# A spectral layer and two MLPs on one core: the second chunk of the first MLP by blocks

## The chip, the cores and the metric

One core of a Trainium2 chip runs the whole program. The metric is the device time of one execution, in microseconds. The kernel before took 1215.2 us (median of three runs, 1214.34 to 1215.99).

## The reference

Three steps follow one another on 2 x 3008 tokens of 256 features, in float32:

```python
X = np.fft.rfft(x, axis=1)                       # over the 3008 tokens
Yr = Xr @ w_r - Xi @ w_i + b_r
Yi = Xr @ w_i + Xi @ w_r + b_i
Yr, Yi = soft_threshold(Yr, 0.01), soft_threshold(Yi, 0.01)
x = np.fft.irfft(Yr + 1j * Yi, n=3008, axis=1)   # to 6016 x 256
h = x @ w_in1;  x = (h * sigmoid(h)) @ w_out1    # 256 -> 2048 -> 256
h = x @ w_in2;  out = max(0.01 * h, h) @ w_out2  # 256 -> 2048 -> 256
```

The MLP weights arrive as float64 words; the kernel reads them as pairs of 32-bit words and rebuilds float32 values on chip.

## The kernel before, in words

**Precision.** Every float32 operand of a matmul is split into a high part (hi, a cast) and a low part (lo, the difference). A product is three matmuls: lo·hi, hi·lo, hi·hi.

**Stages.** A first transform makes a_sb. Then 48 spectral items run, one call of spectrum(j) for each j; the stages of several items overlap in one call (STAGES lists them with their lag, in the order in which each engine gets them): threshold, split_a, split_z, split_y, store, mix, forward, backward. mix writes a PSUM bank pz, forward py, backward pb; store copies pb to SBUF as bo and sends it to a scratch tensor in HBM. inverse reads that back (bt) and writes px, from which the token columns (ring) are split. The last five calls of spectrum lie inside the first iterations of the MLP loop.

**MLP loop.** The tokens are cut into 12 chunks, 11 of 512 and one of 384. Per layer and chunk there are 8 pairs; a pair holds two slices of 128 hidden columns. Iteration i of the loop issues, in program order: for the pair before (one) parts of its preparation; first(0) of pair i; the products "1" of pair i-2 (two); one step of preparation for the next chunk (make_next, a px of the inverse in layer 1); first(1); the products "a" and "b" of pair i-2; the last preparation of pair i-1; and behind all that the weight work (split_w, then sums_w1). Pairs 0 to 7 are chunk 0, 8 to 15 chunk 1, 16 to 23 chunk 2. first(s) is six matmuls of 512 columns into a bank ph.

**Plain and by blocks.** A plain pair splits both activated slices and multiplies them with four 128 x 128 weight blocks: 12 matmuls of 512 columns, issued one iteration later. A pair by blocks uses Strassen's scheme in Winograd's form: seven products of 256 columns instead of eight, each three matmuls, so 21 matmuls of 256 columns, issued two iterations later. It needs sums of the activations (t1 on POOL; t23 and t4 on DVE) and seven weights (S1 to S4, A11, A12, A22). In the kernel before, chunks 0 and 1 of layer 1 are plain and the others by blocks (the last is a tail of its own).

**Weights.** The pieces of the first layer's weights are loaded (L116, wraw), begun (ACT L123 and L125, DVE L128 and L130), scaled (DVE L135), added (POOL L142) and split (ACT L149, POOL L150). In the spectral stage fifth does parts of a piece behind each item; in chunk 0 step does one piece behind each first. The sums of the block weights come later: sums_w1(p) at the end of iteration 8 + p (POOL L470 and four L457), split_w at the end of iteration 9 + p (four casts on ACT, L463; four differences on DVE, L464, called wlo).

**Activation and preparation.** Behind first(s) ACT computes a tanh (L520) and DVE finishes the activation (L521). Of a pair by blocks, POOL makes t1 (L538) and la (L526), DVE t23 (L545), l (L526), t4 (L552) and lb (L526, 768 columns), ACT the casts h, ha and hb (L564).

**Order and waits.** The program fixes the order on every engine as it is written; each engine takes its instructions in that order, and one that waits holds back what stands behind it. All of PSUM is two pools of four banks: ps_h (ph, py, px) and ps_a (pa, pz, pb and the sums acc). A new tile of a pool waits for the readers of the tile whose bank it takes.

Of the kernel before, what the change touches and what calls it, by code (L numbers as in the profile page):

```python
# [9 lines left out]
F32 = mybir.dt.float32  # L10
# [61 lines left out]
def spectral_mlp_kernel(ctx, tc, x, w_r, w_i, b_r, b_i, w_in1, w_out1, w_in2, w_out2, da, ea, dm, out):  # L72
# [7 lines left out]
    near = dict(reuse_waits="tile")  # L80
    dram = pool("dram", 1, space=bass.MemoryType.DRAM)
    ps_h = pool("ps_h", 4, space=bass.MemoryType.PSUM)
    ps_a = pool("ps_a", 4, space=bass.MemoryType.PSUM)
    const = pool("const", 1)
    stage = pool("stage", 3)

# [9 lines left out]
    def weight_pieces(win, wout, in_dst, out_dst):  # L96

        win, wout = win.bitcast(U32), wout.bitcast(U32)
        pieces = []
        for q in range(NF // 2 + 1):
            if q < NF // 2:
                for d in range(2):
                    pieces.append((win[d * 128:(d + 1) * 128, q * 512:(q + 1) * 512], [w[:, d * DFF + q * 256:d * DFF + (q + 1) * 256] for w in in_dst]))
            if q:
                for f in (2 * q - 2, 2 * q - 1):
                    pieces.append((wout[f * 128:(f + 1) * 128, :], [w[:, f * D:(f + 1) * D] for w in out_dst]))
        loaded, begun, scaled, rounded, made = [], [], [], [], []  # L110

        def load():
            if pieces:
                src, dst = pieces.pop(0)
                raw = raws[0].tile([128, 512], F32, tag="wraw", name="wraw", bufs=3 if raws[1:] else 2).bitcast(U32)
                nc.sync.dma_start(out=raw, in_=src)  # L116
                loaded.append((raw.rearrange("p (e w) -> p e w", w=2), dst))

        def begin():
            raw, dst = loaded.pop(0)  # L120
            m = stage.tile([128, 256], U32, tag="wm", name="wm", bufs=2)
            c = stage.tile([128, 256], F32, tag="wc", name="wc", bufs=4).bitcast(U32)
            nc.scalar.activation(out=c, in_=raw[:, :, 0], func=ACTF.Copy, scale=2.0 ** -29)  # L123

            nc.scalar.activation(out=m.bitcast(F32), in_=raw[:, :, 1].bitcast(F32), func=ACTF.Copy, scale=2.0 ** -112)  # L125
            yield

            nc.vector.tensor_scalar(out=m.bitcast(F32), in0=m.bitcast(F32), scalar1=MAG, scalar2=-MAG, op0=ALU.min, op1=ALU.max)  # L128
            yield
            nc.vector.tensor_scalar(out=m, in0=m, scalar1=3, scalar2=0x7FFFFFFF, op0=ALU.logical_shift_left, op1=ALU.bitwise_and)  # L130
            begun.append((raw, m, c, dst))

        def scale():
            raw, m, c, dst = begun.pop(0)
            nc.vector.scalar_tensor_tensor(out=m, in0=raw[:, :, 1], scalar=0x80000000, in1=m, op0=ALU.bitwise_and, op1=ALU.bitwise_or)  # L135
            yield
            scaled.append((m, c, dst))

        def around(add):
            m, c, dst = scaled.pop(0)  # L140
            r = dst[0].bitcast(U32) if len(dst) == 1 else c
            add.tensor_tensor(out=r, in0=c, in1=m, op=ALU.add)  # L142
            rounded.append((c.bitcast(F32), dst))

        def split():
            c, dst = rounded.pop(0)
            if len(dst) == 2:
                hi, lo = dst
                nc.scalar.copy(hi, c)  # L149
                nc.gpsimd.tensor_tensor(out=lo, in0=c, in1=hi.bitcast(F32), op=ALU.subtract)  # L150
            made.append(1)

        def step():

            if scaled:
                around(nc.gpsimd)
            parts = [p() for p, ready in ((scale, begun), (begin, loaded and len(begun) < 2)) if ready]
            done = len(rounded)
            while parts:
                for p in list(parts):  # L160
                    if next(p, parts) is parts:
                        parts.remove(p)
            for _ in range(done):
                split()
            if scaled:
                around(nc.gpsimd)
            load()

        def fifth(i):

            if i in (0, 3):
                if rounded:
                    split()
                if loaded and not begun:
                    list(begin())
            elif i in (1, 4) and begun:
                list(scale())
            if i in (2, 4) and scaled:
                around(nc.gpsimd)
                load()  # L180

        def until(n):
            while len(made) < min(n, 2 * NF):
                step()

        return load, step, fifth, until
# [41 lines left out]
    with tc.tile_pool(name="xp", bufs=6) as xp:  # L228
# [20 lines left out]
            load_x(c)  # L249
        wms = xp.tile([128, 2, 2, D], F32, name="wms", bufs=1)  # L250
        for c in range(R2 // NA):
            pa = [ps_a.tile([128, 512], F32, tag="acc", name="pa") for _ in range(2)]
            for s in range(NA):
                for h in range(2):
                    nc.tensor.matmul(  # L255
                        pa[h][:, s * 128:(s + 1) * 128],
                        lhsT=xt[c][:, s, h * 128:(h + 1) * 128],
                        rhs=da_sb,
                        start=True,
                        stop=True,  # L260
                        skip_group_check=True,
                    )
            xt.pop(c)
            load_x(c + 5)
            for h in range(2):
                (nc.vector.tensor_copy if h and c > 14 else nc.scalar.copy)(
                    a_sb[:, h, :, c * NA:(c + 1) * NA], pa[h].rearrange("p (s j) -> p j s", s=NA)[:, :NJ])
            if c in (6, 7):
                nc.sync.dma_start(out=wms[:, :, c - 6, :], in_=(w_r, w_i)[c - 6].rearrange("(h p) e -> p h e", p=128))
            elif c == 8:  # L270
                braw = xp.tile([128, D], F32, name="braw", bufs=1)
                nc.vector.memset(braw, 0.0)
                for p in (0, 32, 64, 96):
                    nc.sync.dma_start(out=braw[p:p + 1, :], in_=(b_r, b_i)[p // 32 % 2].rearrange("(o e) -> o e", o=1))
                nc.vector.memset(pick.bitcast(F32), 0.0)
                for p in (0, 32, 64, 96):
                    nc.vector.memset(pick[p:p + 1, p // 32 % 2 * 64:][:, :64].bitcast(F32), 1.0)
            elif c == 10:
                load_dm(0)
            elif c == 11:  # L280
                load_dm(2)
            elif c == 12:
                nc.scalar.copy(bias, braw)
                nc.vector.tensor_tensor(out=bias[64:], in0=braw[64:], in1=bias[64:].bitcast(F32), op=ALU.subtract)
                nc.scalar.copy(wm["hi"], wms)
                nc.vector.tensor_tensor(out=wm["lo"], in0=wms, in1=wm["hi"].bitcast(F32), op=ALU.subtract)
                nc.sync.dma_start(out=ea_sb, in_=ea)
            elif c == 13:
                split_dm(0)
            if c > 13:  # L290
                load_w()
# [12 lines left out]

    def mix(j):
        hi, lo = a_t.pop(j)
        pz = ps_a.tile([128, 512], F32, tag="acc", name="pz")
        terms = [(u, v, h) for u, v in ((hi, wm["lo"]), (lo, wm["hi"]), (hi, wm["hi"])) for h in range(2)]
        for n, (u, v, h) in enumerate(terms):
            nc.tensor.matmul(pz, lhsT=u[:, h, :], rhs=v[:, h].rearrange("p g e -> p (g e)"),  # L310
# [12 lines left out]
    def forward(j):  # L323
        zh, zl = z_t.pop(j)
        dh, dl = dm_t[j]
        py = ps_h.tile([128, 512], F32, tag="h", name="py")[:, :D]
        terms = [(u[:, 64 * (1 - g):64 * (3 - g)], v[:, g, :]) for u, v in ((dl, zh), (dh, zl), (dh, zh)) for g in range(2)]
        for n, (u, v) in enumerate([(pick, bias)] + terms):
            nc.tensor.matmul(py, lhsT=u, rhs=v, start=(n == 0), stop=(n == len(terms)))  # L329
# [17 lines left out]
    def backward(j):  # L347
        yh, yl = y_t.pop(j)
        dh, dl = dm_t.pop(j)
        pb = ps_a.tile([128, 512], F32, tag="acc", name="pb")[:, :D]  # L350
        for n, (u, v) in enumerate(((dl, yh), (dh, yl), (dh, yh))):
            nc.tensor.matmul(pb, lhsT=u[:, 192:], rhs=v, start=(n == 0), stop=(n == 2))  # L352
        b_p[j] = pb
# [30 lines left out]
    for j in range(n_items - 1):  # L384
        spectrum(j)
        if j == n_items - KH + KT + 6:
            load_b()
            load_b()
        fifth_w(j % 5)
    right.close()  # L390


# [3 lines left out]
    at = lambda t: t % RING  # L396
    accs, x2f, late = {}, {}, {}

    def inverse(h):

        g, n, bt = bts[0]
        px = ps_h.tile([128, 512], F32, tag="h", name="px")
        for s in range(n):
            nc.tensor.matmul(px[:, s * PAIR:(s + 1) * PAIR], lhsT=bt[:, s, h * 128:(h + 1) * 128],  # L404
                             rhs=ea_sb, start=True, stop=True, skip_group_check=True)
# [25 lines left out]
    def ahead(layer, c):  # L431
# [3 lines left out]
        steps = []  # L435
        while made[0] < sum(CHUNKS[c]):
            made[0] += sizes.pop(0) * PAIR
            steps += [lambda h=h: inverse(h) for h in range(2)]
        return steps


# [41 lines left out]
    class Pair:  # L483
# [4 lines left out]
        def __init__(self, layer, c, p):  # L488
            self.layer, self.c, self.p = layer, c, p
            self.t0, self.n = CHUNKS[c]  # L490
            self.mode = "plain" if layer == 1 and c < 2 else "blocks" if self.n == 512 else "tail"
            self.ph = {}

        def first(self, s):
# [79 lines left out]
        def acc(self, i):  # L574
            key = self.layer, self.c, i
            if key not in accs:
                accs[key] = ps_a.tile([128, 512], F32, tag="acc", name="acc")
            return accs[key]

        def products(self, which):  # L580
# [70 lines left out]
    for i in range(len(pairs) + 2):  # L651
# [9 lines left out]
        def between(f):  # L661
            if f < 10 and f % 2 == 0:
                spectrum(n_items + 1 + f // 2)
            if 0 < f < NF:
                step_w()
            if f == 6:
                raws.pop(0)
            if f == 9:
                fs.close()
                late["m2"] = pool("late", 2, **near)  # L670
                late["m4"] = pool("late4", 2, **near)
# [93 lines left out]
```

## Time and profile before

| | |
|---|---|
| median of the runs | 1215.2 us |
| profiled execution | 1214.85 us |
| its span | 1213.1 us |
| PE busy | 1196.0 us (99%) |
| DVE busy | 842.3 us (69%) |
| ACT busy | 782.3 us (64%) |
| POOL busy | 567.2 us (47%) |

The span runs from the first to the last instruction; the rest of the execution's time lies around it. A busy time is the time in which an engine runs at least one instruction. Matmuls overlap in the pipeline, so the distance between two starts says more than the duration of one. In the trace the MLP loop begins at 167.92 us, chunk 1 at 222.32 us and chunk 2 at 268.90 us.

### The profile page before, as it was taken

The numbers are of one execution on the slowest core, as the hardware profiler recorded it, in microseconds if no ns is written. First come the engines' busy times: TensorE is split into PE (matmuls) and PEld (weight loads), VectorE is DVE, ScalarE is ACT, GpSimd is POOL, SyncE is SP. The second block draws the span as 40 slices with busy tenths as digits, with TensorE's granted clock in tenths as the row PEclk, the third lists the DMA queues.
The fourth block names the chain that finished last, engine by engine and source line by source line (L and its number), as shares of the span: only waits on it lengthen the run. The fifth ranks groups of instructions, "written<-read, shape, count | busy, mean of one in ns | idle before, by whom it ended". The sixth has DMA issues, their size and how long they took to land.

```text
span 1213.1 us, 20072 instructions
## 1 busy us (share of the span) xinstructions
PE 1196.0 (99%) x7346; PEld 1071.5 (88%) x7346; DVE 842.3 (69%) x1525; ACT 782.3 (64%) x1614; POOL 567.2 (47%) x606
## 2 busy tenths in 40 slices
PE   9999998999999999999999999999999999999998
PEld 9888886888999999989999988988888898888898
DVE  0798877768889888888988895555555455555543
ACT  4898866656666666666665776656656665665664
POOL 0334524543444444444545575555545455554532
PEclk9999999999999999999999999999999999999999
DMA  9344443001112111101100110110011011001000
GB/s 218 111 125 129 139 138 101 32 14 48 51 31 64 57 40 49 58 26 55 45 26 19 35 32 1 35 36 31 5 36 36 1 35 36 28 9 35 32 1 31
DMA packets 35882, 61.60 MB, mean 51 GB/s; under 512 B 3908, under 2 KB 15784, under 8 KB 35784
## 3 DMA queue, kind: packets, MB, share of 16 engines
q1 hardware_dynamic: 35784, 60.33, 16.2%
q8 instruction: 57, 0.93, 0.3%
q14 instruction: 41, 0.34, 0.1%
HBM read 41.70 MB, written 18.61 MB: 50 GB/s over the span
## 4 chain that ended last, share of the span: by engine, by line
PE 91%; DVE 3%; ACT 2%; DMA 2%; issue 1%; SPq 0%; ACTq 0%; DVEq 0%
PE ph L501 41%; PE acc L571 37%; PE pz L310 4%; PE py L329 2%; PE pa L255 2%; PE px L404 2%; DVE wlo L464 1%; PE pb L352 1%; DMA wraw<-in_moe_w_out_dram 1%; DMA bt<-scr 0%; ACT bo L358 0%; DMA xt<-in_x_dram 0%; DVE py L337 0%; DVE ph L521 0%; DMA wraw<-in_moe_w_in_dram 0%
## 5 line engine op out<-in xcount | busy, mean ns | idle before, releaser
L526 POOL TENSOR_TENSOR la<-u,ha 128x512 fp32r<-128x512 f32 (+1 forms) x176 | 232.8, 1323 | 246.7 <-ACT ha L564 245.7
L526 DVE TENSOR_TENSOR lb<-u,hb 128x768 fp32r<-128x768 f32 (+1 forms) x176 | 178.2, 1012 | 220.7 <-ACT hb L564 219.0
L501 PE MATMUL ph<-xhi,winlo 128*128 128x512 f32 (+1 forms) x768 | 240.3, 394 | 5.5 <-DVE la L526 5.5
L501 PE MATMUL ph<-xlo,winhi 128*128 128x512 f32 (+1 forms) x768 | 239.1, 391 | 1.2 <-POOL xlo L427 1.2
L501 PE MATMUL ph<-xhi,winhi 128*128 128x512 f32 (+1 forms) x768 | 237.6, 391 | 0.0
L520 ACT ACTIVATE u<-ph 128x512 f32<-128x512 f32 (+1 forms) x192 | 113.8, 593 | 139.2 <-PE ph L501 139.2
L501 PEld LDWEIGHTS ph<-xlo,winhi 128*128 128x128 f32 x768 | 144.0, 188 | 36.3 <-POOL xlo L427 5.5
L501 PEld LDWEIGHTS ph<-xhi,winhi 128*128 128x128 f32 x768 | 143.8, 188 | 30.8
L538 POOL TENSOR_TENSOR u<-u 128x256 f32<-128x256 f32 x160 | 126.0, 787 | 64.9 <-DVE u L521 58.4
L564 ACT CAST hb<-u 128x768 fp32r<-128x768 f32 (+1 forms) x176 | 140.4, 798 | 9.4 <-DVE u L552 4.9
L571 PE MATMUL acc<-lb,whi 128*128 128x256 f32 (+1 forms) x496 | 141.1, 284 | 0.0
L571 PE MATMUL acc<-hb,whi 128*128 128x256 f32 (+1 forms) x496 | 139.6, 281 | 0.0
L571 PE MATMUL acc<-hb,wlo 128*128 128x256 f32 (+1 forms) x496 | 139.5, 281 | 0.0
L501 PEld LDWEIGHTS ph<-xhi,winlo 128*128 128x128 f32 x768 | 120.5, 189 | 9.1 <-DVE la L526 6.2
L523 ACT ACTIVATE ph<-ph 128x512 f32<-128x512 f32 (+1 forms) x96 | 55.1, 574 | 113.0 <-PE ph L501 113.0
L521 DVE SCALAR_TENSOR_TENSOR ph<-u,ph 128x512 f32<-128x512 f32 (+1 forms) x112 | 76.5, 683 | 64.4 <-ACT u L520 64.4
L564 ACT CAST ha<-u 128x512 fp32r<-128x512 f32 (+1 forms) x176 | 109.7, 623 | 14.7 <-POOL u L538 14.7
L526 DVE TENSOR_TENSOR l<-ph,h 128x512 fp32r<-128x512 f32 (+1 forms) x176 | 117.2, 666 | 0.0
L545 DVE TENSOR_TENSOR u<-ph,u 128x512 f32<-128x512 f32 x160 | 109.0, 681 | 6.3 <-POOL u L538 6.3
L564 ACT CAST h<-ph 128x512 fp32r<-128x512 f32 (+1 forms) x176 | 102.4, 582 | 2.7 <-DVE ph L521 1.6
L571 PE MATMUL acc<-ha,whi 128*128 128x256 f32 (+1 forms) x352 | 102.1, 290 | 0.0
L571 PE MATMUL acc<-la,whi 128*128 128x256 f32 (+1 forms) x352 | 100.9, 287 | 0.0
(123 smaller groups left out, 2669.0 us busy)
## 6 DMA issues: line engine op xcount, KB each, us to landing
wraw<-in_moe_w_in_dram SPq DMA_DIRECT2D x32, 256.0 KB
wraw<-in_moe_w_out_dram SPq DMA_DIRECT2D x32, 256.0 KB
scr<-bo SPq DMA_DIRECT2D x48, 128.0 KB
scr<-x2o SPq DMA_DIRECT2D x22, 256.0 KB
x2i<-scr SPq DMA_DIRECT2D x22, 256.0 KB
out_dram<-x2o SPq DMA_DIRECT2D x22, 256.0 KB
dmr<-in_dm_dram SPq DMA_DIRECT2D x34, 160.0 KB
bt<-scr SPq DMA_DIRECT2D x14, 384.0 KB
```

The costliest lines, as they stand in the source:

```text
L255: nc.tensor.matmul(pa[h][:, s * 128:(s + 1) * 128], lhsT=xt[c][:, s, h * 128:(h + 1) * 128], rhs=da_sb, start=True, stop=True, skip_group_ ...
L310: nc.tensor.matmul(pz, lhsT=u[:, h, :], rhs=v[:, h].rearrange("p g e -> p (g e)"), start=(n == 0), stop=(n == len(terms) - 1))
L329: nc.tensor.matmul(py, lhsT=u, rhs=v, start=(n == 0), stop=(n == len(terms)))
L501: nc.tensor.matmul(ph, lhsT=u[:, h, f * 128:(f + 1) * 128], rhs=v[:, h, :], start=(i == 0), stop=(i == len(terms) - 1))
L520: nc.scalar.activation(out=th, in_=ph, func=ACTF.Tanh)
L521: nc.vector.scalar_tensor_tensor(out=out, in0=th, scalar=1.0, in1=ph, op0=ALU.add, op1=ALU.mult)
L523: nc.scalar.activation(out=out, in_=ph, func=ACTF.Prelu, alpha=0.01)
L526: eng.tensor_tensor(out=lo, in0=src, in1=hi.bitcast(F32), op=ALU.subtract)
L538: nc.gpsimd.tensor_tensor(out=blk(1), in0=blk(0), in1=blk(2), op=ALU.subtract)
L545: nc.vector.tensor_tensor(out=v[:, 3:5], in0=b22, in1=v[:, 0:2], op=ALU.subtract)
L564: nc.scalar.copy(hi, src)
L571: nc.tensor.matmul(dst, lhsT=u, rhs=v, start=(begin and self.p == 0 and i == 0), stop=(end and self.p == NF // 2 - 1 and i == 2), skip_gro ...
```

## The change

Chunk 1 of layer 1 goes by blocks. The four banks of ps_a become two pools of two: pa, pz and the sums 0 and 1 take from the first or both, pb, the last py, the px made for chunk 1 and the sums 2 and 3 from the second. There are four early buffers for raw weight words where there were three, with one more load behind item 0, and they are kept until the sixteenth slice of chunk 0. From item 28 on the weight work is spread over three items instead of five (one piece instead of two).

```diff
-    ps_a = pool("ps_a", 4, space=bass.MemoryType.PSUM)
+    ps_a = [pool(f"ps_a{i}", 2, space=bass.MemoryType.PSUM) for i in range(2)]
...
-                raw = raws[0].tile([128, 512], F32, tag="wraw", name="wraw", bufs=3 if raws[1:] else 2).bitcast(U32)
+                raw = raws[0].tile([128, 512], F32, tag="wraw", name="wraw", bufs=4 if raws[1:] else 2).bitcast(U32)
...
-            pa = [ps_a.tile([128, 512], F32, tag="acc", name="pa") for _ in range(2)]
+            pa = [p.tile([128, 512], F32, tag="acc", name="pa") for p in ps_a]
...
-        pz = ps_a.tile([128, 512], F32, tag="acc", name="pz")
+        pz = ps_a[0].tile([128, 512], F32, tag="acc", name="pz")
...
-        py = ps_h.tile([128, 512], F32, tag="h", name="py")[:, :D]
+        at_, tag = (ps_a[1], "acc") if j == len(items) - 1 else (ps_h, "h")
+        py = at_.tile([128, 512], F32, tag=tag, name="py")[:, :D]
...
-        pb = ps_a.tile([128, 512], F32, tag="acc", name="pb")[:, :D]
+        pb = ps_a[1].tile([128, 512], F32, tag="acc", name="pb")[:, :D]
...
-        fifth_w(j % 5)
+        if j == 0:
+            load_w()
+
+        fifth_w(j % 5 if j < 2 * KT else (j - 2 * KT) % 3)
...
-        px = ps_h.tile([128, 512], F32, tag="h", name="px")
+        at_, tag = (ps_a[1], "acc") if c == 1 else (ps_h, "h")
+        px = at_.tile([128, 512], F32, tag=tag, name="px")
...
-            self.mode = "plain" if layer == 1 and c < 2 else "blocks" if self.n == 512 else "tail"
+            self.mode = "plain" if layer == 1 and c == 0 else "blocks" if self.n == 512 else "tail"
...
-                accs[key] = ps_a.tile([128, 512], F32, tag="acc", name="acc")
+                accs[key] = ps_a[i // 2].tile([128, 512], F32, tag="acc", name="acc")
...
-            if f == 6:
+            if f == NF - 1:
                 raws.pop(0)
-            if f == 9:
                 fs.close()
                 late["m2"] = pool("late", 2, **near)
                 late["m4"] = pool("late4", 2, **near)
```

## Rows read from the trace of the kernel before

**Rows 1.** The page's first part: busy time, share of the span, instructions.

```profile
PE 1196.0 (99%) x7346; PEld 1071.5 (88%) x7346; DVE 842.3 (69%) x1525; ACT 782.3 (64%) x1614; POOL 567.2 (47%) x606
```

**Rows 2.** Busy time by stretches: length, engines (instructions), granted clock, DMA share, GB/s.

```profile
112.00:158.00 46.00, 43.56 (x260) 37.85 (x259) 41.21 (x84) 40.44 (x116) 23.89 (x29) 1.00 0.46 137
165.00:222.30 57.30, 51.76 (x255) 42.35 (x254) 41.23 (x84) 35.20 (x89) 19.35 (x26) 1.00 0.30 95
222.30:277.30 55.00, 55.00 (x245) 44.63 (x244) 36.99 (x76) 33.56 (x78) 26.45 (x44) 1.00 0.08 29
```

**Rows 3.** Waits from 165 to 222 us: who for whom, total us, times, longest.

```profile
ACT wc L123 <- DMA wraw<-in_moe_w_out_dram: 11.8, 6, 3.7
...
PE ph L501 <- DVE la L526: 5.5, 4, 2.2
```

**Rows 4.** PE in order of time: start us, duration us, instructions merged as x.

```profile
170.14 0.28 PE L352 MATMUL pb<-yh,dml 128*128 128x256 f32 x1
...
179.53 0.63 PE L501 MATMUL ph<-xhi,winlo 128*128 128x512 f32 x2
...
222.32 0.63 PE L501 MATMUL ph<-xhi,winlo 128*128 128x512 f32 x2
...
252.10 0.63 PE L501 MATMUL ph<-xhi,winlo 128*128 128x512 f32 x2
...
257.70 0.63 PE L501 MATMUL ph<-xhi,winlo 128*128 128x512 f32 x2
...
300.21 0.63 PE L501 MATMUL ph<-xhi,winlo 128*128 128x512 f32 x2
...
303.72 0.28 PE L571 MATMUL acc<-ha,wlo 128*128 128x256 f32 x1
...
305.50 0.63 PE L501 MATMUL ph<-xhi,winlo 128*128 128x512 f32 x2
```

**Rows 5.** ACT and DVE in order of time, a steady iteration of chunk 2.

```profile
304.41 0.83 ACT L564 CAST hb<-u 128x768 fp32r<-128x768 f32 x1
...
305.27 0.96 DVE L526 TENSOR_TENSOR lb<-u,hb 128x768 fp32r<-128x768 f32 x1
306.15 0.42 DVE L135 SCALAR_TENSOR_TENSOR wm<-wraw,wm 128x256 uint32<-128x256 uint32 x1
```

**Rows 6.** DVE and POOL in order of time, split and sums in chunk 1.

```profile
252.09 1.29 DVE L464 TENSOR_TENSOR wlo<-wsum,whi 128x256 fp32r<-128x256 f32 x4
...
253.46 1.30 POOL L470 TENSOR_TENSOR wsum<-wouthi,woutlo 128x512 f32<-128x512 f32 x1 [2.38 <-DVE wlo L464]
254.84 1.84 POOL L457 TENSOR_TENSOR wsum<-wsum 128x128 f32<-128x128 f32 x4
```

**Rows 7.** DVE and POOL near 714 us (layer 2's first pairs); last, all such wlo by form.

```profile
714.89 1.28 DVE L526 TENSOR_TENSOR lb<-u,hb 128x768 fp32r<-128x768 f32 x1 [0.90 <-ACT hb L564]
...
717.50 2.26 DVE L464 TENSOR_TENSOR wlo<-m,whi 128x128 fp32r<-128x128 f32 x2
719.68 0.68 DVE L545 TENSOR_TENSOR u<-ph,u 128x512 f32<-128x512 f32 x1
720.28 0.68 DVE L526 TENSOR_TENSOR l<-ph,h 128x512 fp32r<-128x512 f32 x1
...
713.78 0.73 POOL L538 TENSOR_TENSOR u<-u 128x256 f32<-128x256 f32 x1
...
715.31 1.18 POOL L457 TENSOR_TENSOR wsum<-wsum,m 128x128 f32<-128x128 f32 x1
...
717.43 1.29 POOL L526 TENSOR_TENSOR la<-u,ha 128x512 fp32r<-128x512 f32 x1
...
L464 DVE TENSOR_TENSOR wlo<-wsum,whi 128x256 fp32r<-128x256 f32 x40 | 16.9, 456 | 0.0
```

**Rows 8.** ACT in order of time: the two bo of the loop's first iterations.

```profile
171.47 0.38 ACT L358 COPY bo<-pb 128x256 f32<-128x256 f32 x1
...
177.01 0.38 ACT L358 COPY bo<-pb 128x256 f32<-128x256 f32 x1
```

More of the change, by code (lines that the diff above doesn't have):

```diff
@@ L397, in spectral_mlp_kernel, with inverse @@
     accs, x2f, late = {}, {}, {}
-    def inverse(h):
+    def inverse(h, c):
         g, n, bt = bts[0]
-        px = ps_h.tile([128, 512], F32, tag="h", name="px")
+        at_, tag = (ps_a[1], "acc") if c == 1 else (ps_h, "h")
+        px = at_.tile([128, 512], F32, tag=tag, name="px")
         for s in range(n):
@@ L437, in ahead @@
             made[0] += sizes.pop(0) * PAIR
-            steps += [lambda h=h: inverse(h) for h in range(2)]
+            steps += [lambda h=h: inverse(h, c) for h in range(2)]
         return steps
```

## The prediction

> **What bounds the kernel now.** Read the page's first part, then the busy time by stretches, then the waits of one stretch, then instructions in order of time. PE is busy 99% of the span [rows 1], so a saving off PE counts only where PE waits. By stretches it waits in two places near the change: the last 20 spectral items (43.56 us busy of 46.00) and chunk 0 (51.76 of 57.30); chunk 1 has no idle PE, 55.00 of 55.00 [rows 2]. In chunk 0 PE waited four times, 5.5 us in all, for a hidden-layer bank that DVE had not yet released, while ACT stood 11.8 us before line 123 for raw weights [rows 3]. At a granted clock of 1.00 throughout [rows 2], PE time follows the columns.
>
> **Part 1: chunk 1 by blocks, on PE.** A pair of chunk 1 takes 5.60 us from first matmul to first matmul (252.10 to 257.70); a pair by blocks takes 5.29 (300.21 to 305.50) [rows 4]. Eight pairs save 8 x 0.31 = 2.5 us.
>
> **Part 2: what chunk 1 then waits for.** Its second-layer products need the seven sums of the weights. sums_w1 for pair p runs on POOL at the end of iteration 8+p, split_w on ACT and DVE at the end of 9+p, the products at 10+p. The diff does not move them; but before, nobody read them until iteration 18, and now the last DVE result of one iteration is wanted by PE in the next. Let T be the moment when PE has issued first(1) of an iteration (303.72 in a steady one). PE then has 15 products of 256 columns (1.78) and first(0), and wants S4 and A12 at T + 3.2.
>
> DVE's order behind T is second activation, lb, four wlo. lb starts at T + 1.55 (305.27) and the next instruction 0.88 later; hb before it starts on ACT at T + 0.69 [rows 4, 5]. The four wlo took 1.29 us alone [rows 6], so undisturbed the last is done at T + 3.7, only 0.2 late for the fourth matmul.
>
> They won't be undisturbed. In chunk 1 now, POOL has nothing but the sums, which wait for the split; so L470 and the wlo never overlap (252.09 to 253.38, then 253.46) [rows 6]. By blocks POOL also has t1 (0.73) and la (1.29), which pull the sums beside lb and wlo. Where POOL and DVE both work from SBUF alone the rows show one waiting out the other's whole instruction: two wlo took 2.26 us, beside la (717.43, 1.29) and what followed, instead of 0.5; L457 took 1.18 instead of 0.46 and ended 0.32 us after lb did [rows 7]. DVE's operations that read PSUM are not held (L545, 0.68 beside L457; the next 0.60 later) [rows 7].
>
> The mean of wlo, 456 ns over 40 [rows 7], would say that this hardly costs anything; but 24 of the 40 are chunk 1's, where POOL waits for them. [...]
>
> Worked with exclusion, from chunk 1's first matmul as 0: iteration 8 takes 2.8 of first and 2.8 of plain products, iteration 9 has only its two first (T = 8.4), iteration 10 wants weights at 9.8. DVE has the activation of pair 9 at 8.55, t1 ends at 9.35, L470 runs 9.4 to 10.7. lb, ready at 9.95, waits and ends at 11.6. Then L457 and wlo alternate four times, 0.32 + 0.28 each, so A12 comes at 13.9. Three matmuls (0.36), px (0.81) and first(1) (1.40) end at 16.5; without a wait it were 12.7: **+3.7 us**.
>
> In a steady iteration let W be the end of the last wlo, counted from T. PE's next T comes 0.1 + 0.36 + 1.40 = 1.86 behind W. DVE does t23, l, t4 and the first activation behind W (0.60 + 0.60 + 0.34 + 0.60, so 2.2), which ends at the next T + 0.3. Then t1 to 1.1, L470 to 2.45, lb to 3.35, four alternations to W = 5.6. The iteration takes 5.6 + 1.86 = 7.4 instead of 5.29: +2.1 in each of iterations 13 to 16. In 11 and 12 the px of the iteration before gives DVE 0.81 us of lead, W is 4.7: +1.2 each. In 17 no sums run: +0.2. Together 3.7 + 2.4 + 8.4 + 0.2 = 14.7 us of new waits. POOL's own load (1.29 + 0.73 + 1.30 + 1.84 = 5.2) and DVE's lb and wlo (2.1) come to 7.3 a pair, so the loop and the shared resource say the same. Bounds: +2.7 (no exclusion: A12 at 12.1, so 2.0 in iteration 10, and 0.1 in each of the seven behind it) and +18 (each wlo waits for a whole L457 of 0.46). I take 14.7, since the stretch at 714 us is the nearest row: the same pairs, by blocks, with sums and split beside them. Net of part 1: **+12.2**.
>
> **Part 3: chunk 0, banks and early buffers.** px of chunk 1 and the last py leave ps_h, so PE no longer finds that bank taken by pair p-1: the four waits go. The fourth early buffer with the load at j == 0 puts each raw weight one load ahead, so line 123 finds it landed, and SP's blocking behind the stores of bo no longer matters. What is late next is ps_a[1], two banks for pb, py and px. The last py takes one, pb of item 45 needs the other, which bo of item 44 frees: bo runs 171.47 to 171.85 [rows 8], pb ran at 170.14 [rows 4]. PE loses 1.8 us there, first(1) and its activation come that much later. pb of item 46 then needs the bank of pb 45 or of the last py, freed by the second bo or the yl beside it: in the trace of before 177.01 to 177.39 [rows 8], now about 178.9, while PE would be ready for it at 175.1. Behind it on PE wait first(1) and the products of pair 0, whose end moves from 179.53 [rows 4] to about 183.5: +4.0. From there to 222.32 PE took 42.8 us for 37.2 of matmuls; with the waits gone and 0.6 for px (behind bo 46) it takes 37.8: −5.0. Sum **−1.0**, between −6.3 (the banks of ps_a[1] free in time) and +4.0 (DVE, 41.23 of 57.30 busy, sets the pace after all).
>
> **Part 4: the spectral items.** Items 28 to 46 begin a weight piece every third item instead of twice in five: 7 begins instead of 8. The 46.00 us stretch with its 2.44 us of idle PE [rows 2] held 6 to 7 begins, about 0.35 each. One fewer, less the lateness of the piece that moves to chunk 0 and of pz waiting for zl where it waited for bo: **−0.5**, between −2.4 (all idle time goes) and +1.5. The pools for the first transform and the later time of fs.close change no order: nothing, since ACT and PE have no wait on them in the trace; if a late tile had to wait for an early buffer, it would be the last piece's scale, under 1 us.
>
> **Sum.** 1214.85 us is the profiled execution (span 1213.1 and 1.75 around it). +12.2 − 1.0 − 0.5 gives 1225.6; the median shown, 1215.2, lies 0.35 higher: **1226 us**.
>
> **The rivals.** *No exclusion of weight* (chance 0.14): wlo stays at 0.32 each, chunk 1 costs 2.7 − 2.5 = 0.2, and 1215.2 + 0.2 − 1.5 leaves 1214. For it: the mean of wlo; against it: the stretch at 714 us. *The banks free and the weights early* (0.08): the mechanism is ps_h. If every new wait on ps_a[1] is hidden and the sums run ahead because POOL's t1 finds them done, chunk 0 gives 5 and chunk 1 2.5: 1215.2 − 7.5 − 0.5 = 1207. It decides from the point where the last wlo ends before T + 3.2. For it: 5.5 us of PE waits in rows 3; against it: the order on POOL. [...] *More than the loop* (0.06): the +4.0 of chunk 0 is not won back, or each wlo waits a whole L457: 1231 to 1235. *The forecast* holds 0.72, its own range 1220 to 1231.
>
> **How the numbers follow.** About 0.2% (2.4 us) is what a measurement of this kernel tells from no change. Slower: forecast and the third rival, with a little of the first's upper end, 0.79. Same: most of the first, 0.12. Faster: 0.09. The range for 8 in 10 reaches down to the first rival, 1213, and up to 1232.
>
> **What would show it.** In the trace after: PE waiting for DVE wlo (line 464 of before) at the products "1" of chunk 1, seven or eight times, 1 to 4 us each; iterations of chunk 1 some 7.4 us apart; wlo and lb far over 0.42 and 0.96 us; pb waiting for bo twice near 171 and 175; no wait of line 123 for a DMA in chunk 0. If PE runs chunk 1 at 5.3 to 5.4 us a pair, part 2 is wrong; if the products of pair 0 end near 179, part 3 is.

## The result and the profile after

The changed kernel takes 1228.87 us (median of 5, 1228.52 to 1230.01) where the kernel before takes 1215.2: a ratio of 1.0112, 95% interval 1.0101 to 1.0124. It is slower by 13.7 us. The profiled execution took 1228.82 us with a span of 1227.0, 13.9 more than the span before, and its page begins so (against [rows 1]):

```profile
PE 1203.1 (98%) x7418; PEld 1077.8 (88%) x7418; DVE 857.2 (70%) x1545; ACT 788.2 (64%) x1624; POOL 592.0 (48%) x624
```

PE has 7 us more of busy time, though blocks have fewer columns to multiply. The same stretches as in [rows 2] (cut a little differently, since chunk 1 starts at 223.68 now) say why. The columns are length, busy time of the engines, granted clock, DMA share and GB/s:

```profile
165.00:222.00 57.00, 50.56 (x237) 41.51 (x237) 39.80 (x84) 35.72 (x89) 19.51 (x26) 0.94 0.30 90
222.00:277.30 55.30, 48.04 (x247) 39.55 (x247) 44.96 (x76) 30.43 (x69) 44.05 (x55) 0.94 0.05 18
```

In chunk 1 PE is idle for 7.3 us of 55.3, where it was never idle; POOL goes from 26.45 to 44.05 us, DVE from 36.99 to 44.96. And the granted clock, 1.00 in both stretches before, is 0.94. Shorter stretches of the same view show where:

```profile
170.00:176.50 6.50, 3.42 (x15) 2.54 (x15) 3.52 (x7) 3.69 (x9) 0.72 (x1) 1.00 0.24 67
176.60:183.40 6.80, 5.13 (x14) 4.16 (x15) 3.17 (x9) 3.12 (x10) 1.50 (x2) 0.50 0.35 99
...
238.10:241.40 3.30, 3.30 (x12) 2.82 (x12) 1.89 (x5) 0.63 (x2) 2.57 (x3) 0.50 0.02 5
...
255.10:258.40 3.30, 3.30 (x14) 3.01 (x13) 2.04 (x4) 1.78 (x4) 2.23 (x3) 0.50 0.00 0
```

In three stretches the granted clock is 0.50, called the lower clock from here on; around them it is 1.00. The first begins inside a wait of PE of 4.17 us (at 176.57), the others 1.6 and 1.1 us behind the ends of waits of 2.77 (ended 236.42) and 1.25 us (ended 253.94). PE's waits from 165 to 300 us, in place of the one for la in [rows 3], are:

```profile
PE acc L577 <- DVE wlo L470: 8.5, 10, 2.8
PE pb L353 <- ACT bo L359: 5.8, 2, 4.2
PE px L410 <- ACT bo L359: 0.7, 1, 0.7
```

and PE in order of time, where [rows 4] showed it before:

```profile
170.68 0.39 PE L353 MATMUL pb<-yh,dml 128*128 128x256 f32 x1 [1.60 <-ACT bo L359]
...
178.27 0.58 PE L353 MATMUL pb<-yh,dml 128*128 128x256 f32 x1 [4.17 <-ACT bo L359]
...
179.08 1.05 PE L507 MATMUL ph<-xhi,winlo 128*128 128x512 f32 x2
179.93 1.05 PE L507 MATMUL ph<-xlo,winhi 128*128 128x512 f32 x2
...
185.24 0.63 PE L507 MATMUL ph<-xhi,winlo 128*128 128x512 f32 x2
...
223.68 0.63 PE L507 MATMUL ph<-xhi,winlo 128*128 128x512 f32 x2
...
236.42 0.39 PE L577 MATMUL acc<-h,wlo 128*128 128x256 f32 x1 [2.77 <-DVE wlo L470]
...
271.64 0.62 PE L507 MATMUL ph<-xhi,winlo 128*128 128x512 f32 x2
...
274.21 0.39 PE L577 MATMUL acc<-h,wlo 128*128 128x256 f32 x1 [1.01 <-DVE wlo L470]
...
275.01 0.39 PE L577 MATMUL acc<-h,wlo 128*128 128x256 f32 x1 [0.18 <-DVE wlo L470]
...
278.63 0.63 PE L507 MATMUL ph<-xhi,winlo 128*128 128x512 f32 x2
```

Two 512-column matmuls take 0.85 us from start to start at 179.08, at a granted clock of 0.50, and 0.46 at 185.24, at 1.00 (185.24 to 185.70). From 271.64 to 278.63 an iteration of chunk 1 takes 6.99 us, at a granted clock of 1.00. What DVE and POOL do in it (compare [rows 5 to 7]):

```profile
271.42 1.55 DVE L532 TENSOR_TENSOR lb<-u,hb 128x768 fp32r<-128x768 f32 x1
272.89 2.07 DVE L470 TENSOR_TENSOR wlo<-wsum,whi 128x256 fp32r<-128x256 f32 x4
274.88 0.68 DVE L551 TENSOR_TENSOR u<-ph,u 128x512 f32<-128x512 f32 x1
275.48 0.67 DVE L532 TENSOR_TENSOR l<-ph,h 128x512 fp32r<-128x512 f32 x1
```

```profile
270.85 1.30 POOL L476 TENSOR_TENSOR wsum<-wouthi,woutlo 128x512 f32<-128x512 f32 x1
272.23 3.04 POOL L463 TENSOR_TENSOR wsum<-wsum 128x128 f32<-128x128 f32 x4
275.23 1.29 POOL L532 TENSOR_TENSOR la<-u,ha 128x512 fp32r<-128x512 f32 x1
```

Beside the sums, lb takes 1.55 us (0.96 before), the four wlo 2.07 (1.29), and POOL's four small sums 3.04 (1.84). The two operations that read ph, which is in PSUM, take 0.68 and 0.67 beside la, as in [rows 7].

By stages, from starts of PE's matmuls (before, then after): the first matmul of the loop 167.92 and 166.69; iterations 0 and 1, 11.61 and 18.54; 2 to 7, 42.79 and 38.45; 8 to 19, 67.33 and 79.93; the rest 920.01 and 920.02. So chunk 0 lost 2.6 us and chunk 1 12.6. The mark of the loop itself scatters: over the 14 profiled executions of this study it lies between 166.4 and 169.1, with and without the early buffers. But most of that scatter lies ahead of the first pz; from the first matmul of pz to the loop's first it is 131.8 us before and 130.9 after, so the spectral items gained some 0.9 us.

### The profile page after: what moved, and what is told of

Read it like the earlier page. It is cut to its first block, busy times and chain, and to the rows that moved or that the text cites. A ratio compares the mean times of both kernels' runs of the same rounds, so it can differ in the third digit from the quotient of the medians.

```text
span 1227.0 us, 20275 instructions
## 1 busy us (share of the span) xinstructions
PE 1203.1 (98%) x7418; PEld 1077.8 (88%) x7418; DVE 857.2 (70%) x1545; ACT 788.2 (64%) x1624; POOL 592.0 (48%) x624
## 4 chain that ended last, share of the span: by engine, by line
PE 92%; DVE 4%; ACT 2%; issue 1%; POOL 1%; DVEq 0%; ACTq 0%; POOLq 0%
PE ph L507 42%; PE acc L577 37%; PE pz L310 5%; PE py L330 2%; PE pa L255 2%; PE px L410 2%; DVE wlo L470 1%; PE pb L353 1%; DVE wm L128 1%; DVE zl L320 0%; PE warm L246 0%; DVE py L338 0%; DVE lb L532 0%; ACT u L526 0%; ACT hb L570 0%
## 5 line engine op out<-in xcount | busy, mean ns | idle before, releaser
L532 POOL TENSOR_TENSOR la<-u,ha 128x512 fp32r<-128x512 f32 (+1 forms) x184 | 243.0, 1321 | 245.7 <-ACT ha L570 244.9
L532 DVE TENSOR_TENSOR lb<-u,hb 128x768 fp32r<-128x768 f32 (+1 forms) x184 | 188.4, 1024 | 221.0 <-ACT hb L570 219.0
L544 POOL TENSOR_TENSOR u<-u 128x256 f32<-128x256 f32 x168 | 131.8, 785 | 68.7 <-DVE u L527 62.2
L570 ACT CAST hb<-u 128x768 fp32r<-128x768 f32 (+1 forms) x184 | 147.0, 799 | 9.3 <-DVE u L558 4.9
L577 PE MATMUL acc<-lb,whi 128*128 128x256 f32 (+1 forms) x520 | 148.0, 285 | 0.0
L577 PE MATMUL acc<-hb,whi 128*128 128x256 f32 (+1 forms) x520 | 146.4, 282 | 0.0
L577 PE MATMUL acc<-hb,wlo 128*128 128x256 f32 (+1 forms) x520 | 146.4, 282 | 0.0
L570 ACT CAST ha<-u 128x512 fp32r<-128x512 f32 (+1 forms) x184 | 114.7, 624 | 14.7 <-POOL u L544 14.7
L527 DVE SCALAR_TENSOR_TENSOR ph<-u,ph 128x512 f32<-128x512 f32 (+1 forms) x104 | 71.1, 683 | 71.2 <-ACT u L526 71.1
L551 DVE TENSOR_TENSOR u<-ph,u 128x512 f32<-128x512 f32 x168 | 114.5, 681 | 6.5 <-POOL u L544 6.3
L577 PE MATMUL acc<-h,wlo 128*128 128x256 f32 (+1 forms) x352 | 101.2, 288 | 9.0 <-DVE wlo L470 8.5
```

The source lines that it names most:

```text
L527: nc.vector.scalar_tensor_tensor(out=out, in0=th, scalar=1.0, in1=ph, op0=ALU.add, op1=ALU.mult)
L532: eng.tensor_tensor(out=lo, in0=src, in1=hi.bitcast(F32), op=ALU.subtract)
L544: nc.gpsimd.tensor_tensor(out=blk(1), in0=blk(0), in1=blk(2), op=ALU.subtract)
L551: nc.vector.tensor_tensor(out=v[:, 3:5], in0=b22, in1=v[:, 0:2], op=ALU.subtract)
L570: nc.scalar.copy(hi, src)
L577: nc.tensor.matmul(dst, lhsT=u, rhs=v, start=(begin and self.p == 0 and i == 0), stop=(end and self.p == NF // 2 - 1 and i == 2), skip_gro ...
```

## The experiments

All are timed in 5 rounds beside the kernel before. Times by stage, in us, from the starts of PE's matmuls in the profiled executions:

| kernel | median | ratio to before, 95% | iterations 0–1 | 2–7 | 8–19 | rest |
|---|---|---|---|---|---|---|
| before | 1215.2 | | 11.61 | 42.79 | 67.33 | 920.01 |
| after | 1228.87 | 1.0101–1.0124 | 18.54 | 38.45 | 79.93 | 920.02 |
| e1 blocks only | 1228.13 | 1.0085–1.0111 | 11.60 | 42.68 | 80.65 | 920.00 |
| e2 rest only | 1216.9 | 0.9999–1.0016 | 17.76 | 38.45 | 67.33 | 920.04 |
| e3 no sums | 1218.8 | 1.0016–1.0034 | 17.77 | 38.45 | 69.30 | 919.42 |
| e4 last py | 1224.26 | 1.0055–1.0079 | 11.79 | 38.85 | 80.64 | 920.06 |
| e5 one earlier | 1224.34 | 1.0051–1.0079 | 18.54 | 38.46 | 73.45 | 921.65 |
| e6 loose sums | 1231.59 | 1.0115–1.0143 | 18.55 | 38.45 | 79.98 | 921.74 |
| e7 rest, py | 1211.74 | 0.9947–0.9975 | 11.78 | 38.88 | 67.31 | 921.82 |
| e8 earlier, py | 1217.56 | 1.0004–1.0021 | 11.80 | 38.86 | 73.42 | 921.80 |
| e9 light port | 1214.98 | 0.9982–1.0000 | 11.78 | 38.85 | 70.61 | 920.05 |
| e10 la on DVE | 1220.4 | 1.0021–1.0046 | 11.78 | 38.85 | 77.06 | 920.07 |
| e11 e7 again | 1210.51 | 0.9937–0.9965 | 11.78 | 38.89 | 67.31 | 920.03 |
| e12 sums after la | 1223.19 | 1.0042–1.0073 | 11.79 | 38.85 | 80.21 | 920.04 |

The last column is 920.0 or 921.7. The larger value has a stretch at the lower clock between 703 and 723 us; e7 has it (0.50 from 702.90 to 706.20) and e11, the same kernel, has not (1.00 from 700 to 710). It is not a matter of the edits and is left out of the comparisons by stage. The stage 8–19 holds stretches at the lower clock too: two of 3.4 us in the changed kernel and e6, one of 6.8 in e1 and e4, one of 3.4 in e5, e8, e10 and e12, none in the others (mean granted clock from 218 to 300 us: 0.96 in e1, e4 and e6, 0.98 in e5, e8, e10 and e12, 1.00 in e3, e7 and e9).

**The change in two halves.** e1 makes the one edit in the kernel before, e2 takes it back in the changed one:

```
-  self.mode = "plain" if layer == 1 and c < 2 else ...     # e1; e2 the reverse,
+  self.mode = "plain" if layer == 1 and c == 0 else ...    # with chunk 1's acc in ps_a[1]
```

> The kernel before with its second chunk by blocks and nothing else of the change. Theory A (the weights of a pair come one iteration too late because GpSimd's sums and VectorE's SBUF subtractions exclude each other; banks and buffers have no part in it): chunk 1 loses its whole +12.6 us here too, about 1227.8 us (1225.5 to 1230), and TensorE's waits in it are for the low halves of the weights. Rival D (the new split of the banks or the early buffers make chunk 1 slow): under 1222 us.

> The changed kernel with its second chunk plain again, so that only the early buffers, the pace of the weight loads and the banks are left of the change. Theory A: chunk 1 as before, the spectral layer -1.2 us and chunk 0 +2.6 us, together 1216.6 us (1215.2 to 1218). Rival D: most of the loss stays, over 1222 us.

e1 loses 13.3 us in chunk 1 and nothing elsewhere; e2 loses nothing in chunk 1 and 1.8 in chunk 0 (17.76 + 38.45 against 11.61 + 42.79; its stretch at the lower clock there is 3.4 us long, the changed kernel's 6.8; e3, with 17.77 us in iterations 0 and 1, has a mean granted clock of 0.97 from 165 to 218 us, e5, with 18.54, of 0.94). The two halves don't act on each other, and rival D is out. e1's waits from 165 to 310 us show both bottlenecks side by side, the new one and the old one of chunk 0 that the banks were to remove:

```profile
PE acc L571 <- DVE wlo L464: 9.5, 11, 2.8
PE ph L501 <- DVE la L526: 5.5, 4, 2.2
```

**Chunk 0: the last py.**

```
-  at_, tag = (ps_a[1], "acc") if j == len(items) - 1 else (ps_h, "h")
+  at_, tag = ps_h, "h"
```

> The changed kernel with the last py (item 47) back in the four banks of ps_h. Theory A (py 47 and the pb share two banks, so pb 46 waits for the copy bo, and the half clock follows from that wait): the 4.2 us wait of pb 46 goes, TensorE stays at full clock in the first two iterations, 1.5 to 5 us less than the changed kernel, 1224 to 1227.3 us. Rival E (the wait is only moved, to a first matmul in ps_h or to a later pb): within 1 us of the changed kernel.

Iterations 0 and 1 fall from 18.54 to 11.79 us, and only 0.4 us of it come back later (38.85 against 38.45). The waits of pb are gone, and so is the lower clock:

```profile
165.00:222.00 57.00, 54.58 (x269) 44.98 (x269) 44.01 (x91) 38.86 (x97) 23.09 (x31) 1.00 0.32 95
```

So the change of chunk 0 was good but for that one line: without it, chunk 0 is 3.8 us shorter than before (50.64 against 54.40).

**Chunk 1: are the sums to blame?** e3 leaves them out, so the weights of the blocks in layer 1 are not those of the reference:

```
-  r = stage.tile(...); hi, lo = ...; nc.gpsimd.tensor_tensor(out=r, in0=hi, in1=lo, op=ALU.add)
-  sums_w(p, r)
+  r = hold["w"]["hi"][:, p * 512:(p + 1) * 512].bitcast(F32)
+  halves.extend((u, p, i) for i, u in ((S1, r[:, :256]), (S3, r[:, 256:512]), (A11, r[:, :128]), (A12, r[:, 256:512])))
```

> The changed kernel without the five sums of each pair on GpSimd in chunk 1; the splits of the weights stay and read the stored high halves instead (so the weights of the blocks in layer 1 are not the right ones). Theory A: the low halves of the weights take 0.28 to 0.42 us each, TensorE doesn't wait for them, an iteration takes 5.3 to 5.6 us, chunk 1 is 10 to 12.5 us shorter than in the changed kernel and no stretch of it is at the half clock: 1217 to 1219 us. Rival B (the blocks themselves, their order and their long path from activation to product, not the sums): iterations stay at 6 to 7 us, 1224 us or more.

Chunk 1 is 10.6 us shorter than in the changed kernel, at a clock of 1.00 throughout:

```profile
222.00:277.30 55.30, 53.63 (x303) 44.64 (x302) 46.02 (x93) 37.95 (x86) 20.37 (x22) 1.00 0.05 17
```

It is still 2.0 us longer than chunk 1 plain. PE has one wait of 1.7 us at the start, and in each steady iteration PE's loads of S4 and A12 wait for the second and the fourth wlo, though nothing disturbs DVE. A DVE stretch in order of time, and the first of the two loads:

```profile
258.62 1.29 DVE L470 TENSOR_TENSOR wlo<-wouthi,whi 128x256 fp32r<-128x256 f32 x4
259.83 0.68 DVE L549 TENSOR_TENSOR u<-ph,u 128x512 f32<-128x512 f32 x1
```

```profile
259.43 0.19 PEld L575 LDWEIGHTS acc<-h,wlo 128*128 128x128 f32 x1 [0.34 <-DVE wlo L470]
```

Iterations take 5.60 to 5.65 us, just what plain ones take. The saving of 0.31 a pair is not seen in any of these iterations.

**Chain or shared resource?** e6 keeps the sums as work on POOL but lets the splits read the stored halves (weights as in e3), so no split waits for a sum:

```
   sums_w(p, r)
+  halves.clear(); r = hold["w"]["hi"][...]; halves.extend(...)      # as in e3
```

> The changed kernel with GpSimd's five sums in their place, but with the splits reading the stored high halves as if there were no sums (so the weights of the blocks in layer 1 are not the right ones): the same work on GpSimd, without the chain from sum to split. Theory A2 (taking turns): low halves of 0.67 us and iterations of 6.3 to 7 us remain, 1222 us or more. Theory A1 (the chain of latencies): as without the sums, 1217 to 1219 us, iterations of 5.6 us.

Chunk 1 takes 79.98 us against 79.93, with waits equal to the changed kernel's in number and size and the same DVE rows:

```profile
272.12 1.55 DVE L535 TENSOR_TENSOR lb<-u,hb 128x768 fp32r<-128x768 f32 x1
273.59 2.07 DVE L470 TENSOR_TENSOR wlo<-wouthi,whi 128x256 fp32r<-128x256 f32 x4
275.58 0.68 DVE L554 TENSOR_TENSOR u<-ph,u 128x512 f32<-128x512 f32 x1
```

That nobody needs the sums changes nothing: it is their running beside lb and wlo that costs. Together with e3 this shows that the sums stretch DVE's work, and it rules out the chain from sum to split. e5 gives a head start of one iteration, which lets PE go on without the wlo of the moment:

```
-  if k <= i <= NF:       split_w();  if i < NF: sums_w1(i - k)
+  if k - 1 <= i < NF:    split_w();  if i < NF - 1: sums_w1(i - k + 1)
```

> The changed kernel with the sums and the splits of a pair's weights of chunk 1 one iteration earlier (the first sums at the end of iteration 7), so that a pair's low halves are due one iteration after they are made. Theory A1 (a loop of latencies: sums, split and product each hand on one iteration later, just too late): TensorE's waits for the low halves go, iterations 5.6 us, 1216.5 to 1219 us. Theory A2 (throughput: in one pair GpSimd's sums 3.1, la 1.3 and t1 0.7 us and VectorE's low halves 1.5 and lb 1.0 us take turns, 7.6 us against TensorE's 5.6): the head start hides only part of the shortage, iterations of 6.5 to 7 us come back within the chunk, 1221 to 1225 us.

The waits for wlo go, and iterations 12 and 13 take 5.29 us: the saving of blocks is there when the weights are early. But iterations 15 and 16 take 6.88, and in them DVE has no idle time at all (the window ends at 274.8, so the last row shows two of the four wlo):

```profile
266.48 3.19 DVE L470 TENSOR_TENSOR wlo<-wsum,whi 128x256 fp32r<-128x256 f32 x4
269.58 0.68 DVE L551 TENSOR_TENSOR u<-ph,u 128x512 f32<-128x512 f32 x1
...
272.30 1.12 DVE L532 TENSOR_TENSOR lb<-u,hb 128x768 fp32r<-128x768 f32 x1
273.34 2.12 DVE L470 TENSOR_TENSOR wlo<-wsum,whi 128x256 fp32r<-128x256 f32 x2
```

PE waits for l and u instead. That is A2's outcome (a shortage, not a latency), 4.5 us better than the changed kernel and 6.5 in chunk 1.

**Both improvements, and blocks again.** e7 is e2 with the edit of e4; e8 is e5 with it.

> The rest of the change with chunk 1 plain and the last py in ps_h: both improvements that the runs so far point to. Chunk 0 3.8 us shorter than before (as in e4_last_py), chunk 1 as before, the spectral layer at most 0.5 us less: 1211 to 1212.5 us, faster than both kernels. Rival E (what chunk 0 gains is given back in chunk 1): 1214.5 us or more.

> The changed kernel with the last py in ps_h and the sums and splits of chunk 1 one iteration earlier: e7_rest_py with blocks in chunk 1. Theory A1: 1211.5 to 1214 us (the 2.5 us of fewer products are lost again to weight loads that follow a wait, 0.33 us an iteration). Theory A2: 5 to 9 us over e7_rest_py, 1216.5 to 1221 us.

> e7_rest_py once more, on the chip of the two runs beside it, so that chunk 1 plain and by blocks can be compared: 1210.5 to 1212.5 us.

e7 beats both kernels: 1211.74 and in e11 1210.51 us, 0.4 to 0.5% less than before. The gains of chunk 0 stay in (50.66 us, 3.7 less than before), the spectral items keep their 0.9, chunk 1 is as before. e8 is 5.8 us slower than e7; in chunk 1 alone it loses 6.1.

**Taking load off.** If turns at the shared resource were all, less of either engine's work should shorten the iteration.

```
-  one.low("a", nc.gpsimd)                                                                  # e9 and e10
+  one.low("a", nc.vector if (one.layer, one.c) == (1, 1) else nc.gpsimd)
   # e9 also: for A11 and A12 (with A22), instead of the split
+  nc.scalar.copy(hi, stored_hi); nc.scalar.copy(lo, stored_lo)
```

> e8_earlier_py with less on the shared side in chunk 1: la moves from GpSimd to VectorE, and of the blocks A11, A12 and A22 ScalarE copies the high and low halves that are already stored, so that VectorE makes two low halves of a pair and not four. Theory A2 in spacings of the changed kernel (sums 2.9, la 1.25, t1 0.7, low halves 1.2, lb 0.9, together 6.95 us, the period seen was 6.9 to 7.0): now 2.9 + 0.6 + 0.7 + 0.65 + 0.9 = 5.75 us a pair, with the head start of one iteration enough for eight pairs: iterations of 5.3 to 5.8 us, chunk 1 at least 4.5 us shorter than in e8_earlier_py, 1209.5 to 1213 us. Against it (the limit is something else, ScalarE or VectorE's own queue): over 1215 us.

> e8_earlier_py with la of chunk 1 on VectorE and nothing else: theory A2 gives 6.95 - 1.25 + 0.6 = 6.3 us a pair, between e8_earlier_py and e9_light_port: 1212.5 to 1215.5 us. Against it: as e8_earlier_py, 1217 us or more.

Both miss. e10 is slower than e8, with iterations of 7.30 us; e9 is faster, but its 6.23 us are 0.5 over the sum. DVE in e10, from one first wlo to the next (here and in e9 the last row is cut off by the window's end):

```profile
260.05 3.18 DVE L470 TENSOR_TENSOR wlo<-wsum,whi 128x256 fp32r<-128x256 f32 x4
263.15 0.68 DVE L551 TENSOR_TENSOR u<-ph,u 128x512 f32<-128x512 f32 x1
263.76 0.67 DVE L532 TENSOR_TENSOR l<-ph,h 128x512 fp32r<-128x512 f32 x1
264.35 0.41 DVE L558 TENSOR_TENSOR u<-u,ph 128x256 f32<-128x256 f32 x1
264.68 0.67 DVE L527 SCALAR_TENSOR_TENSOR u<-u,ph 128x512 f32<-128x512 f32 x1
265.28 0.68 DVE L532 TENSOR_TENSOR la<-u,ha 128x512 fp32r<-128x512 f32 x1
265.88 0.68 DVE L527 SCALAR_TENSOR_TENSOR ph<-u,ph 128x512 f32<-128x512 f32 x1
266.48 0.95 DVE L532 TENSOR_TENSOR lb<-u,hb 128x768 fp32r<-128x768 f32 x1
267.35 1.51 DVE L470 TENSOR_TENSOR wlo<-wsum,whi 128x256 fp32r<-128x256 f32 x1
```

and in e9:

```profile
258.07 2.11 DVE L474 TENSOR_TENSOR wlo<-wsum,whi 128x256 fp32r<-128x256 f32 x2
260.10 0.68 DVE L558 TENSOR_TENSOR u<-ph,u 128x512 f32<-128x512 f32 x1
...
264.30 1.51 DVE L474 TENSOR_TENSOR wlo<-wsum,whi 128x256 fp32r<-128x256 f32 x1
```

In steady iterations of both, DVE has no idle time, and starts follow one another closely, so a count from start to start has to close; what it shows is where the time goes, which A2 had not told. Undisturbed, DVE needs 1.21 us for four wlo (258.62 to 259.83 in e3), 2.73 for the five operations that read PSUM (263.15 to 266.48 in e10, without la's 0.60) and 0.87 for lb: 4.81 a pair. e10 adds 0.60 for la and loses 3.10 − 1.21 = 1.89 in the wlo: 7.30, the iteration seen. e5: 4.81 + 1.89 + 0.17 in lb = 6.87 (seen 6.88). e9 has two wlo fewer (0.54) and la more, and its two wlo take 2.03 instead of 0.67: 4.81 − 0.54 + 0.60 + 1.36 = 6.23, as seen. So with the head start DVE's own queue is the bound (theory A3, put down before the last run), and its four wlo take 1.89 us longer a pair in e5 and e10, with POOL's sums, than in e3 without them. Moving la off POOL took only lb's 0.17 us away. That la had run beside DVE's PSUM operations is the author's reading; in the changed kernel it does, and they take 0.68, 0.67 and 0.40 us (la 275.23 to 276.52). On DVE it was 0.60 us more.

The last run puts the sums where DVE reads PSUM:

```
   one.low("a", nc.gpsimd)
+  if NF // 2 <= i < NF: sums_w1(i - NF // 2)        # and no sums at the end of the iteration
   # t1 of chunk 1 on VectorE; A11, A12 and A22 copied by ScalarE as in e9; last py in ps_h
```

> The changed kernel with the last py in ps_h and three edits in chunk 1: GpSimd makes the sums right behind la, in the middle of the iteration, t1 goes to VectorE, and the stored halves of A11, A12 and A22 are copied by ScalarE as in e9_light_port. After e10_la_dve the theory is A3: VectorE's own queue is the bound, and it stands still only where one of its operations on SBUF alone meets one of GpSimd (1.1 us beside the 512-wide sum, 0.26 beside each 128-wide one); its operations that read PSUM run beside GpSimd at their full pace. Here VectorE has 4.81 - 0.55 + 0.33 = 4.6 us of its own a pair, and the sums meet mostly operations that read PSUM: stalls of 0.3 to 1.0 us, iterations of 5.3 to 5.7 us, 1209.5 to 1213 us. Rival A2 (every us of GpSimd and every us of VectorE on SBUF count, wherever they stand: sums 2.9, la 1.25, t1 0.3, low halves 0.65, lb 0.9, together 6.0 us): as e9_light_port, 1214 us or more.

A miss again, 7.75 us an iteration, and not by either theory. The wlo are undisturbed now (0.42 each), but ACT stands:

```profile
264.11 0.95 ACT L473 CAST whi<-wsum 128x256 fp32r<-128x256 f32 x2 [2.79 <-POOL wsum L463]
264.96 0.29 ACT L470 CAST whi<-wouthi 128x128 fp32r<-128x128 f32 x1
...
265.97 0.57 ACT L577 CAST h<-ph 128x512 fp32r<-128x512 f32 x1
266.45 0.62 ACT L577 CAST ha<-u 128x512 fp32r<-128x512 f32 x1
```

The split on ACT waits for sums of the same iteration; h and ha of the next pair are queued behind it; la on POOL waits for ha, and the next sums are queued behind la. It is a loop through two queues that e12 itself made, so beyond the undisturbed wlo it says little on A3.

## Why the prediction was right, and where it wasn't

The forecast of 1226 us, slower by the loop in chunk 1, held within its own range; nearly all of what it missed lies in part 3 (+2.6 us for −1.0). Step by step:

- **The mechanism of part 2 held.** By iteration, new time over blocks without waits (6.17 us with px, 5.29 without), predicted and measured:

| iteration | 10 | 11 | 12 | 13 | 14–16, each | 17 | sum |
|---|---|---|---|---|---|---|---|
| predicted | 3.7 | 1.2 | 1.2 | 2.1 | 2.1 | 0.2 | 14.7 |
| measured | 5.06 | 0.35 | 3.98 | 0.24 | 1.7 | 0.34 | 15.1 |

The steady iteration goes through the forecast steps one by one and is 7.0 us, not 7.4. From T = 269.86 us, t1 ends at 1.0 (forecast 1.1), L476 at 2.3 (2.45), lb at 3.1 (3.35) and the last wlo at 5.1 (5.6); the next T comes 1.9 behind that (1.86). What was sized too high is the turn of one small sum and one wlo: 0.50 us where the prediction had 0.32 + 0.28. By those numbers its own sum would have been 5.75 and not 5.6, and 14.0 for 13.9 in iteration 10.

That the sums agree so closely, 14.7 and 15.1, is in part luck, since iterations 10 to 13 differ one by one. The lower clock, which was in no term, takes about 1.6 us in iteration 10 (px and first(1) in 3.87 us, 2.29 in iteration 11) and 1.5 in 12. In the iteration behind each stretch PE waits less than forecast: in 11 the sums are over (243.23) before lb has done much (begun 243.09), so lb and wlo run undisturbed (0.96 and 1.28 us), and in 13 PE comes late enough to find the wlo nearly done. For 12 and 13 e1 shows what the clock cost in the end. Its granted clock there is 1.00, the changed kernel's 0.88, and both take the same time (e1 first):

```profile
248.60:263.34 14.74, 11.63 (x68) 9.45 (x67) 13.45 (x21) 7.89 (x20) 11.39 (x14) 1.00 0.00 0
249.83:264.63 14.80, 12.87 (x68) 10.90 (x67) 12.89 (x21) 7.99 (x20) 11.44 (x14) 0.88 0.01 1
```

So the slower matmuls took the place of a wait. For 10 and 11 no kernel with this chunk 1 ran at 1.00, and how much of the 1.6 us stayed is open.

- **That DVE's and POOL's operations on SBUF alone hold each other up, which the prediction took from [rows 7], held.** In the changed kernel they take longer side by side (four wlo 2.07 for 1.29 us, lb 1.55 for 0.96, four small sums 3.04 for 1.84; wlo and lb the same in e6 with the dependence gone), and DVE's 512-column operations with an operand in PSUM keep their 0.68 us beside la (274.88 and 275.48).
- **Part 1, −2.5 us, is right as a saving of PE's work (5.29 us an iteration in 12 and 13 of e5), but no run had it as a whole.** Even with no sums (e3) the wlo come just late for PE, 0.33 us in each steady iteration where the prediction had 0.1; with 2.1 in iteration 10, chunk 1 is 2.0 us longer than plain. The first rival's 1214 us was therefore too low: with no sums to hold anything up the changed kernel takes 1218.8, and of the 4.8 us between them 1.8 are chunk 1's and 2.8 chunk 0's.
- **Part 3 failed in sign: +2.6 us where −1.0 was forecast.** Its pieces were named rightly. pb of item 45 and of item 46 wait for bo (they start 4.0 and 11.6 us behind the loop's first matmul; forecast 3.9 and 11.0), the four waits for la are gone (iterations 2 to 7 gain 4.3, forecast 5.0). The step that failed is "+4.0" for the end of iteration 1: it came 6.9 later. Of the 2.9 us more, 0.6 are the later pb of item 46, and some 2.3 are the lower clock: from 176.57 to 183.40, in and behind the 4.2 us wait, it was at 0.50, which was in no term (from 178.27 to 183.61 PE's matmuls took 5.3 us, at the starts measured at 1.00 some 3.0). In e4 both go together.
- **Part 4, −0.5 us, was right in sign and mechanism; it measures −0.6 to −1.1.** The stretch from the first matmul of pz to the first of the loop takes 131.8 and 131.6 us in the kernel before and e1, and 130.7 to 130.9 in the twelve others, which have the early buffers and the new pace. From 112 to 158 us PE's idle time falls from 2.44 to 1.03: four waits of pz for bo (2.1 us) are gone, and six for zl (1.0) stand there, as was forecast. The items from 27 on gain about 2 us and those ahead of them lose about 1.2; where that loss comes from no run separates.
- **That line 123 would no longer wait for a DMA in chunk 0 was right.** Of its 11.8 us for the second-layer weights [rows 3], and 3.0 more for a first-layer piece, nothing is left in the trace after.

What stays open: whether chunk 1 by blocks can gain its 2.5 us at all, say with the sums made during chunk 0. It wasn't tried, since the sums of eight pairs would need room that the two buffers don't give.

## What to carry to other kernels

Before work is moved to "idle" engines, list for each pair of VectorE and GpSimd operations that will now overlap whether both work on SBUF alone: here four wlo took 2.07 us beside the sums instead of 1.29, and 3.19 in e5. VectorE's queue with these stalls (4.81 + 2.06 us in e5) is what had to fit under TensorE's iteration (5.29). When a bank moves to another pool, follow its new neighbour's release on the last item as well as in the steady state; one line of it cost 6.4 us of chunk 0 here (56.99 against 50.64). Where a wait of some us is added to TensorE, look at the granted clock in and behind it as well as at the wait, and ask whether the engine that sets the pace makes room for it: the 0.50 cost some 2.3 us in iteration 1 here, and the mean of 0.88 nothing over iterations 12 and 13.

## What the runs showed of the hardware

In the changed kernel the granted clock was 0.50 from 176.57 us on, inside a wait of PE of 4.2 us, from 238.0, behind one of 2.8, and from 255.1, behind waits of 0.67 and 1.25. How long a wait was doesn't tell whether the clock fell. From 218 to 300 us its mean was 0.98 in e12, e10, e5 and e8, with longest waits of 2.5, 2.4, 1.9 and 1.9 us; it stayed at 1.00 with the 2.2 us of the kernel before [rows 2 and 3] and with the 1.7 us in e3's chunk 1. Where it was 0.50 and PE fully busy (3.30 of 3.30, from 238.10), 512-column matmuls started 0.43 us apart (two in 0.85, 239.93 to 240.78) instead of 0.23. What brings the clock down no run showed.

In e10 POOL's 512-wide sum, begun at 259.23 us beside an lb of DVE (259.18, one iteration of 7.30 ahead of the one at 266.48), took 2.05 us instead of 1.30, and the first wlo behind an lb took 1.51 (at 267.35) instead of 0.42 (the median of all wlo of the kernel before). By these lengths the sum at 259.23 ended as if it had begun when lb was done (about 260.0), and the wlo at 260.05 as if it had begun when the sum was (261.3): here each engine waited out the other's operation.
